# Grouped-query attention, twice, on one core: each step's maximum over all keys by a GpSimd all-reduce across partitions

## The chip, the cores and the metric

The kernel runs on one core of a Trainium2 chip. The metric is the device time of one execution, in microseconds (us), from the runs shown below. A core has five engines with queues of their own: TensorE (PE in the profile; its weight loads are PEld), VectorE (DVE), ScalarE (ACT), GpSimd (POOL) and SyncE (SP, which here only issues transfers). Each works through its instructions in the order in which they were written, and waits on semaphores for what other engines make.

## The reference

Two independent attention blocks, A and B, of the same shapes; the outputs stand side by side in the last dimension.

```python
# B, Sq, D = 16, 80, 576;  Hq, Hkv, Sk, Dh = 32, 16, 512, 128;  all bfloat16
q = (x @ wq).reshape(B, Sq, Hq, Dh).transpose(0, 2, 1, 3)
k = jnp.repeat(k_cache, 2, axis=1)          # two query heads share one key head
v = jnp.repeat(v_cache, 2, axis=1)
scores = jnp.einsum("bhqd,bhkd->bhqk", q, k) * (Dh ** -0.5)
p = softmax(scores, axis=-1)
o = jnp.einsum("bhqk,bhkd->bhqd", p, v)
return o.transpose(0, 2, 1, 3).reshape(B, Sq, Hq * Dh) @ wo
```

## The kernel before, in words

*Steps.* The work is cut into 128 steps. A step is one block (A or B), one batch row and a group of four key heads, with the eight query heads that belong to them. Its scores are 16 pieces: for each of four key heads and each quarter of the 512 keys, 128 keys on the partitions and 160 columns (two query heads of 80 queries). Three pieces share a PSUM bank, so a piece of work of the score stage is 480 columns wide, and there are 683 of them.

*Score stage.* Line 704 multiplies keys by queries into a bank. Line 710 (VectorE) takes, on each partition, the negated maximum of the bank's columns into a column of `negmax`. Line 714 (ScalarE) makes the exponentials with this as bias, into `p_sb`, which has 27 slots. So the exponentials of each partition, which is a key, have a maximum of their own, and this has to be made good before they are summed over keys.

*The weights of a step, which the change touches.* The 16 pieces of a step lie in 6 columns of `negmax`. Line 736 (VectorE) takes the minimum of these 6 on each partition, `gmin`. Line 739 (TensorE) multiplies `gmin`, repeated over 128 columns as weights, by the identity: each row of the result holds the values of all 128 partitions. Line 743 (VectorE) takes the minimum along this row, `gmn`, which is the same on all partitions: minus the maximum over all keys of the step. Line 746 (ScalarE) makes the six weights per partition, `wt`, by an exponential of `gmn` minus `negmax`. Line 749 (GpSimd) copies the weights as an 18-column strip into `vp`, which gives the sums of the softmax. Line 767 scales V by the weights into `vp`, up to six instructions a step, on GpSimd but for three in the last step (VectorE). `vp` has four slots, the weights two.

*Behind it.* Lines 800 and 819 multiply the exponentials by `vp`; line 839 takes reciprocals of the sums; lines 844 and 849 scale; line 866 transposes; lines 877 and 879 copy to `oT`; line 949 makes the output projection, and lines 961, 969 and 976 gather it. Line 607 makes the queries (from `wq`), and lines 623 and 625 copy them.

*Loads.* K comes by transposing transfers on SP's queue (line 672, five slots), V by plain ones on ScalarE's queue (line 676; the first four on SP's), asked for four steps ahead, when a slot has come free. `wo` and `wq` come on SP's queue.

*What sets the order.* A planner (class `_Sched`) gets every operation with a due time (`key`), a lead (`ahead`) and a duration (`dur`, `lat`), plays them through engine by engine, and writes down the order of each engine; at the same time it gives out PSUM banks, and for operations with two possible engines it picks one. The chip then follows this order, with semaphores between engines. An operation with another duration or on another engine therefore moves others as well. GpSimd's instructions are written for the chip in this order; configuration instructions for it are added when the program is built, and stand in no line of the kernel.

At the end a flag is read on every engine; if sums left the allowed range, a second, plain version of the whole would run. It does not run on these inputs.

Of the kernel before, what the change touches and what calls it, by code (L numbers as in the profile page):

```python
# [1 line left out]

# [3 lines left out]

BF16 = mybir.dt.bfloat16
F32 = mybir.dt.float32
I32 = mybir.dt.int32
AF = mybir.ActivationFunctionType  # L10
AX = mybir.AxisListType
# [7 lines left out]
NNM = 48  # L19
# [42 lines left out]
STENG = "sp"  # L62
STL = 6.0
TLG = 2
TLA = 4.0
TLN = 5
TLO = 4.0
# [12 lines left out]
RCO = 2.0  # L80
# [23 lines left out]
def _mm(n, cols):  # L104
    return n * (cols * MM1 + MM0)
# [271 lines left out]
def bass_concat_heads__gqa_block_cached__gqa_block_cached__near_ridge_kernel(  # L377
# [10 lines left out]
    _, G, SK, DH = A_k_cache.shape  # L388
# [15 lines left out]
    with ExitStack() as es:  # L404
        block = es.enter_context(nc.Block())
        sb = lambda name, shape, dt: es.enter_context(nc.sbuf_tensor(name, shape, dt))
        ident = sb("ident", [128, 128], BF16)
# [10 lines left out]
        osb = sb("osb", [128, NOSB, DC], BF16)  # L418
        acc = sb("acc", [128, NPP * NRT, D], F32)
        negmax = sb("negmax", [128, NNM], F32)  # L420
        gmin = sb("gmin", [128, 2], BF16)
        gmn = sb("gmn", [128, 2], F32)
        wt = sb("wt", [128, 2, 6], F32)
        rinv = sb("rinv", [128, NRI * 5], F32)
# [5 lines left out]
        ps = es.enter_context(nc.psum_tensor("ps", [128, 8, 512], F32))  # L430
# [14 lines left out]
        S = _Sched()  # L445

        def R(res, ver):
            return (res, ver)
# [37 lines left out]
        def em_warmend(e):  # L486
# [5 lines left out]
              stream="warmset")  # L492
        IDENT = R(("ident",), 0)
# [10 lines left out]
        for half in range(NPP):  # L504
            x_ap = probs[0][0]
            for part, (k0, k1) in enumerate(XP):
                def em_ldx(e, x_ap=x_ap, half=half, k0=k0, k1=k1):
# [5 lines left out]
                      writes=[R(("xs", half * NRT + k_), 0) for k_ in range(k0, k1)], dsem="d_x%d%d" % (half, part), land=LAND["x%d%d" % (half, part)],  # L513
                      name="ldx%d.%d" % (half, part), stream="first", dur=0.5, cost=XC * (k1 - k0))
            for blk in range(NRT):
# [11 lines left out]
                def em_xev(e, en=None, half=half, blk=blk, vb=vb):  # L527
# [4 lines left out]
                      stream="X", dur=_mm(5, 128), lat=0.2, alloc=[vb])  # L532
                S.add(("act", "dve") if half else "act" if blk in (1, 3) else "dve", x + 0.3, em_xev, reads=[R(vb, 0)], writes=[R(("xT", half, blk), 0)],
                      name="xev%d" % rb, stream="xed" if half else "xea" if rb in (1, 3) else "xev",
                      dur=dict(act=0.52, dve=0.40), lat=0.13)

        for half in range(NPP):
            x_ap = probs[1][0]
            st0 = UPR + 8 * half - lead[NG // 2 + half]
            for ck in range(5):  # L540
                def em_ldxt(e, x_ap=x_ap, half=half, ck=ck):
# [6 lines left out]
                      writes=[R(("xT", half, b_), 1) for b_ in range(NRT)] if ck == 0 else [R(("xT", half, "t", ck), 1)],  # L548
# [7 lines left out]
        for goct in range(NG):  # L556
# [6 lines left out]
            for pi, (c0, c1) in enumerate(pieces):  # L563
# [11 lines left out]
                for j, (k0, k1, n0, n1) in enumerate(parts):  # L575
                    def em_ldw(e, wq_ap=wq_ap, q=q, wsl=wsl, n0=n0, n1=n1, k0=k0, k1=k1):
                        if k0 == 4:
# [15 lines left out]
            for i in range(8):  # L593
                for c in range(2):
# [6 lines left out]
                    n0, n1 = b0 * SQ, (b0 + nb) * SQ  # L601
# [27 lines left out]
                    if prob:  # L629
                        xr += [R(("xT", half, "t", ck), 1) for ck in range(1, 5)]  # L630
                    S.add("pe", x, em_qp,
                          reads=[R(("wq", wsl, w_, i // 2), wv) for w_ in range(5)] + [R(("wqz",), 0)] + xr,
                          writes=[R(vb, 0)] + [R(("qT", qpos(goct, bl), i), goct) for bl in range(b0, b0 + nb)],
                          name="qp%d.%d.%d" % (goct, i, c), stream="Q" if goct > 1 else "Q%d" % goct,
                          dur=_mm(5, n1 - n0), lat=0.2, alloc=[vb])
                    S.add(("act", "dve"), x + 0.4, em_qev, reads=[R(vb, 0)],
                          writes=[R(("qT", qpos(goct, bl), i), goct) for bl in range(b0, b0 + nb)],
                          name="qev%d.%d.%d" % (goct, i, c), stream="qev" if goct > 1 else "qev%d" % goct,
                          dur=QEV[n1 - n0] if qpos(goct, b0) + nb <= NQS else QEV[n1 - n0, 2])

        for Q in range(NQ):
# [3 lines left out]
            for wc in range(NWC):  # L645
                def em_ldwo(e, wo_ap=wo_ap, h0=q * HH + wc * hc, s0=Q % 2 * HH + wc * hc, hc=hc):
# [5 lines left out]
                      writes=[R(("wo", Q % 2, wc), Q)] + ([R(("warm",), 3), R(("ones",), 1)] if Q + wc == 0 else []),  # L652
# [10 lines left out]
        for U in range(NSU):  # L663
# [10 lines left out]
            def em_ldv(e, vc_ap=vc_ap, b=b, q=q, vs=vs):  # L674
# [7 lines left out]
                  writes=[R(("V", vs), U)],  # L682
# [4 lines left out]
        for t in range(NT):  # L687
            blks = []
            for B_ in range(3 * t, min(3 * t + 3, NBK)):
                U, r_ = divmod(B_, 16)  # L690
# [22 lines left out]
            def em_exp(e, vb=vb, si=si, sl=sl, n=n):  # L713
# [3 lines left out]
                  dur=_mm(len(blks), 160), lat=0.2, alloc=[vb])  # L717
            S.add("dve", kq(t) + 0.45, em_max, reads=[R(vb, 0)], writes=[R(("nm", si), t)],
                  name="max%d" % t, stream="max", dur=0.045 + n * 0.00108, lat=0.12, ahead=MXO)
            S.add("act", kq(t) + 1.1, em_exp, reads=[R(vb, 0), R(("nm", si), t)], writes=[R(("P", sl), t)],  # L720
                  name="exp%d" % t, stream="exp", dur=0.045 + n * 0.00106, lat=0.2)
# [3 lines left out]
        for U in range(NSU):  # L725
            pi, grp = of_step[U]
            vr, vs, gs = U % NV, U % NVP, U % 2
            t0 = PT0[U]
            off = 16 * U - 3 * t0
            n0 = t0 % NNM  # L730
            kg = kq(t0 + 5)
            tla = TLA if U >= NSU - TLG else 0.0
            vbx = S.bank("X")

            def em_g(e, gs=gs, n0=n0):
                return e.tensor_reduce(gmin[:, gs:gs + 1], negmax[:, n0:n0 + 6], axis=AX.X, op=AluOpType.min)

            def em_mb(e, gs=gs, vbx=vbx):
                return e.matmul(ps[:, vbx.phys, 0:128], lhsT=gmin[:, gs:gs + 1].broadcast_to([128, 128]), rhs=ident[:],  # L739
                                start=True, stop=True)  # L740

            def em_mm(e, gs=gs, vbx=vbx):
                return e.tensor_reduce(gmn[:, gs:gs + 1], ps[:, vbx.phys, 0:128], axis=AX.X, op=AluOpType.min)  # L743

            def em_w(e, gs=gs, n0=n0, vs=vs):
                return e.activation(wt[:, gs, :], negmax[:, n0:n0 + 6], AF.Exp, bias=gmn[:, gs:gs + 1], scale=-1.0)  # L746

            def em_wc(e, gs=gs, vs=vs):
                return e.tensor_copy(vp[:, vs, :, 128:129].rearrange("p (r i) o -> p r (i o)", i=3),  # L749
# [1 line left out]

            S.add("dve", kg + 1.0, em_g, reads=[R(("nm", (t0 + i) % NNM), t0 + i) for i in range(6)],
                  writes=[R(("gm", gs), U)], name="g%d" % U, stream="g", dur=0.07, lat=0.13, ahead=RCO + tla)
            S.add("pe", kg + 1.1, em_mb, reads=[R(("gm", gs), U), IDENT], writes=[R(vbx, 0)], name="mb%d" % U,
                  stream="G", dur=_mm(1, 128), lat=0.2, alloc=[vbx], ahead=RCO + tla)
            S.add("dve", kg + 1.2, em_mm, reads=[R(vbx, 0)], writes=[R(("gn", gs), U)], name="mm%d" % U, stream="mm",
                  dur=0.2, lat=0.13, ahead=RCO + 2.0 + tla)
            S.add("act", kg + 1.3, em_w, reads=[R(("gn", gs), U)] + [R(("nm", (t0 + i) % NNM), t0 + i) for i in range(6)],
                  writes=[R(("w", gs), U)], name="w%d" % U, stream="w", dur=0.195, lat=0.15, ahead=RCO + 2.0 + tla)
            S.add("pool", kg + 1.45, em_wc, reads=[R(("w", gs), U)], writes=[R(("vp", vs, "c"), U)], name="wc%d" % U,  # L760
                  stream="vsp", dur=0.167, lat=0.1)
            for r in range(6):
# [7 lines left out]
                def em_va(e, p0=p0, p1=p1, vr=vr, vs=vs, off=off, gs=gs, r=r):  # L770
# [5 lines left out]
                      reads=[R(("w", gs), U), R(("V", vr), U)], writes=[R(("vp", vs, r), U)], name="vs%d.%d" % (U, r),  # L776
                      stream="vs" + ve, dur=dict(p=0.241 + 0.107 * (p1 - p0), d=0.3, a=0.05 + 0.13 * (p1 - p0))[ve],
                      lat=0.1, ahead=0.0 if ve == "p" else 3.0)

            if U == grp[0]:  # L780
                gn = len(grp)
# [10 lines left out]
            for u in range(4):  # L792
# [3 lines left out]
                def em_pv(e, u=u, vo=vo, c0=c0, vs=vs, where=where):  # L796
# [10 lines left out]
                    reads=[R(("P", (t0 + r_) % NPS), t0 + r_) for r_ in rs_] + [R(("vp", vs, r_), U) for r_ in rs_ + ["c"]],  # L807
                    writes=[R(vo, 0)], name="pv%d.%d" % (U, u), stream="PV", dur=_mm(4, 129), lat=0.2,
                    alloc=[vo] if m_ % 3 == 0 else [])
# [3 lines left out]
            def em_pr(e, od=oba[-1], pair=tuple(pair)):  # L813
                last = None
                for h_, (U_, vs_, t0_, where_) in enumerate(pair):
# [10 lines left out]
                  reads=[R(("P", (t0_ + r_) % NPS), t0_ + r_) for _, _, t0_, _ in pair for r_ in range(6)]  # L826
                  + [R(("vp", vs_, r_), U_) for U_, vs_, _, _ in pair for r_ in [0, 1, 2, 3, 4, 5, "c"]],
                  writes=[R(oba[-1], 0)], name="pr%d" % U, stream="PV", dur=0.225 * gn, lat=0.2, mode=1, alloc=[oba[-1]])
# [5 lines left out]
            for h_, (a_, b_, xo) in enumerate(parts_):  # L834
# [6 lines left out]
                def em_on(e, en, pi=pi, r0=r0, vo=vo, a_=a_, b_=b_):  # L841
# [6 lines left out]
                    for k in range(a_, b_):  # L848
# [5 lines left out]
                      stream="rcp", dur=0.08, lat=0.13, ahead=RCO + tlo)  # L854
# [66 lines left out]
        def em_flag(e, vf=vf):  # L921
# [4 lines left out]
              stream="chk", dur=0.1)  # L926
# [269 lines left out]
```

## Time and profile before

| what | value |
|---|---|
| median of 2 runs | 698.87 us (698.3 to 699.44) |
| profiled execution, its own time | 699.79 us |
| its span, first to last instruction | 698.0 us |
| TensorE clock granted | 1.000 |
| bytes moved by DMA | 160.78 MB, mean 230 GB/s |
| read from HBM | 87.46 MB |

The span is what the profile's views divide up; 1.8 us of the profiled execution's time lie around it. A row of a group gives line, engine, operation, what is written from what, the shape and the count, then after the bar the busy time in us, the mean of one in ns, after the next bar the idle time of the engine just before these instructions, and what ended it. Busy times of one engine can overlap by a little, since an instruction may start before the record of the one ahead of it has ended. Matmul ends are modelled, and spans on GpSimd are rough.

### The profile page before, as it was taken

How to read it: one execution, taken by the hardware profiler on the slowest of the kernel's cores; microseconds unless marked ns; L12 is line 12 of the kernel's file. 1: busy time of each engine (PE TensorE's matmuls, PEld its weight loads, DVE VectorE, ACT ScalarE, POOL GpSimd, SP SyncE). 2: the span in 40 equal slices, each digit the busy share in tenths (PEclk: the TensorE clock that was granted, in tenths of full speed). 3: DMA queues.
4: the chain of work that ended last, by engine and by line, in shares of the span. 5: the costliest groups of instructions: out<-in, count | busy, mean ns of one | idle time of the engine just before them, and what ended most of it. 6: DMA issues, size and time to landing. Idle time of an engine off the chain costs nothing.

```text
span 698.0 us, 23763 instructions
## 1 busy us (share of the span) xinstructions
PE 687.7 (99%) x9533; PEld 581.0 (83%) x9533; DVE 650.2 (93%) x1656; ACT 603.8 (86%) x1365; POOL 428.5 (61%) x901
## 2 busy tenths in 40 slices
PE   8999999999999999999999999999999999999996
PEld 5778888888888888888888888888888888888885
DVE  5899889899999999999999999999999999999995
ACT  2778799799999888899989999999898989988893
POOL 1465466656666666567666575666766667675572
PEclk9999999999999999999999999999999999999999
DMA  9999999999999999999999999999999999999951
GB/s 242 210 276 249 258 235 278 223 180 234 244 231 251 231 246 284 225 248 241 243 225 239 253 240 254 234 253 236 226 226 250 231 226 239 222 249 208 197 138 39
DMA packets 362837, 160.78 MB, mean 230 GB/s; under 512 B 276832, under 2 KB 359264, under 8 KB 362720
## 3 DMA queue, kind: packets, MB, share of 16 engines
q1 hardware_dynamic: 297168, 94.10, 76.0%
q10 hardware_dynamic: 65552, 65.09, 31.4%
q8 instruction: 77, 1.26, 0.7%
q14 instruction: 40, 0.33, 0.2%
HBM read 87.46 MB, written 2.95 MB: 130 GB/s over the span
## 4 chain that ended last, share of the span: by engine, by line
PE 89%; DVE 6%; ACT 2%; SPq 2%; DMA 1%; issue 0%
PE ps L607 23%; PE ps L949 21%; PE ps L704 19%; PE ps L800 16%; PE ps L866 5%; PE ps L819 4%; DVE negmax L710 4%; SPq L672 1%; PE ps L739 1%; ACT p_sb L714 1%; DMA acc<-in_A_x_dram 1%; DVE acc L969 0%; ACT o_sb L849 0%; DVE osb L976 0%; DVE o_sb L844 0%
## 5 line engine op out<-in xcount | busy, mean ns | idle before, releaser
L714 ACT ACTIVATE p_sb<-ps,negmax 128x480 bf16<-128x480 f32 (+1 forms) x683 | 421.6, 680 | 46.1 <-DVE negmax L710 43.4
L710 DVE TENSOR_REDUCE negmax<-ps 128x1 f32<-128x480 f32 (+1 forms) x683 | 418.3, 646 | 7.2 <-PE ps L704 6.1
L767 POOL TENSOR_SCALAR vp<-v_sb,wt 128x384 bf16<-128x384 bf16 (+2 forms) x765 | 405.5, 555 | 0.0
L704 PE MATMUL ps<-qT,kT 128*128 128x160 bf16 x2048 | 235.4, 232 | 0.2 <-ACT p_sb L714 0.2
L607 PE MATMUL ps<-xT,wq_sb 128*128 128x320 bf16 (+2 forms) x1280 | 212.2, 299 | 1.4 <-DVE xT L528 0.6
L800 PE MATMUL ps<-vp,p_sb 128*128 128x129 bf16 x2048 | 193.6, 220 | 0.5 <-DVE oT L877 0.2
L749 POOL CAST vp<-wt 128x18 bf16<-128x18 f32 x128 | 33.8, 264 | 258.1 <-ACT wt L746 257.8
L949 PE MATMUL ps<-wo_sb,oT 128*128 128x288 bf16 x1280 | 190.7, 286 | 0.1
L704 PEld LDWEIGHTS ps<-qT,kT 128*128 128x128 bf16 x2048 | 157.4, 97 | 18.3 <-ACT p_sb L714 0.4
L800 PEld LDWEIGHTS ps<-vp,p_sb 128*128 128x128 bf16 x2048 | 142.9, 98 | 10.2 <-DVE oT L877 0.4
L607 PEld LDWEIGHTS ps<-xT,wq_sb 128*128 128x128 bf16 x1280 | 115.3, 98 | 36.0 <-DVE wo_sb L487 0.9
L949 PEld LDWEIGHTS ps<-wo_sb,oT 128*128 128x128 bf16 x1280 | 117.6, 98 | 24.3 <-ACT p_sb L714 0.3
L849 ACT ACTIVATE o_sb<-ps,rinv 128x128 bf16<-128x128 f32 x343 | 101.7, 379 | 5.3 <-DVE rinv L839 4.4
L625 DVE TENSOR_SCALAR qT<-ps 128x320 bf16<-128x320 f32 (+4 forms) x192 | 82.7, 442 | 9.0 <-PE ps L607 7.4
L844 DVE TENSOR_TENSOR o_sb<-ps,rinv 128x384 bf16<-128x384 f32 x100 | 54.8, 548 | 1.5
L877 ACT COPY oT<-ps 128x640 bf16<-128x640 bf16 (+2 forms) x70 | 45.2, 670 | 7.2 <-PE ps L866 6.8
L866 PE MATMUL ps<-ident,o_sb 128*128 128x128 bf16 x640 | 50.2, 219 | 0.6 <-ACT oT L877 0.3
L746 ACT ACTIVATE wt<-negmax,gmn 128x6 f32<-128x6 f32 x128 | 40.3, 315 | 9.0 <-DVE gmn L743 8.3
L866 PEld LDWEIGHTS ps<-ident,o_sb 128*128 128x128 bf16 x640 | 39.8, 98 | 4.1 <-ACT o_sb L849 0.7
L623 ACT ACTIVATE qT<-ps 128x320 bf16<-128x320 f32 (+3 forms) x88 | 37.4, 432 | 6.5 <-PE ps L607 6.0
L969 DVE TENSOR_TENSOR acc<-ps,acc 128x288 f32<-128x288 f32 x80 | 36.1, 451 | 4.8 <-PE ps L949 4.1
L839 DVE RECIPROCAL rinv<-ps 128x3 f32<-128x3 f32 (+1 forms) x216 | 35.7, 169 | 5.2 <-PE ps L800 2.5
(36 smaller groups left out, 259.1 us busy)
## 6 DMA issues: line engine op xcount, KB each, us to landing
v_sb<-in_B_v_cache_dram ACTq DMA_DIRECT2D x64, 512.0 KB, 5.6
v_sb<-in_A_v_cache_dram ACTq DMA_DIRECT2D x60, 512.0 KB, 5.6
wo_sb<-in_A_wo_dram SPq DMA_DIRECT2D x16, 288.0 KB, 5.5
wo_sb<-in_B_wo_dram SPq DMA_DIRECT2D x16, 288.0 KB, 5.7
wq_sb<-in_B_wq_dram SPq DMA_DIRECT2D x16, 256.0 KB, 4.9
out_dram<-osb SPq DMA_DIRECT2D x40, 72.0 KB, 3.8
wq_sb<-in_A_wq_dram SPq DMA_DIRECT2D x4, 512.0 KB, 5.6
v_sb<-in_A_v_cache_dram SPq DMA_DIRECT2D x4, 512.0 KB, 5.6
```

What stands on the lines that cost most here:

```text
L607: last = e.matmul(ps[:, vb.phys, 0:n1 - n0], lhsT=wq_sb[:, wsl, ck, i * 128:(i + 1) * 128], rhs=xT[:, half, ck, n0:n1], start=(ck == 0), s ...
L625: r_ = e.tensor_scalar(dst, src[:, s0:s0 + n_, :], SCALE, None, op0=AluOpType.mult)
L704: last = e.matmul(ps[:, vb.phys, i * 160:(i + 1) * 160], lhsT=kT[:, U % NK, j, u * 128:(u + 1) * 128], rhs=qT[:, qpos(U // 8, U % 8), u * ...
L710: return e.tensor_reduce(negmax[:, si:si + 1], ps[:, vb.phys, 0:n], axis=AX.X, op=AluOpType.max, negate=True)
L714: return e.activation(p_sb[:, sl, 0:n], ps[:, vb.phys, 0:n], AF.Exp, bias=negmax[:, si:si + 1], scale=1.0)
L767: return e.tensor_scalar(vp[:, vs, p0:p1, 0:128], src, wt[:, gs, r:r + 1], 1.0, op0=AluOpType.mult, op1=AluOpType.mult)
L800: last = e.matmul(ps[:, vo.phys, c0:c0 + 129], lhsT=p_sb[:, sl, i * 160:i * 160 + 128], rhs=vp[:, vs, p_, 0:129], start=(j == 0), stop=(j ...
L844: return e.tensor_tensor(o_sb[:, pi % NOS, a_:b_, :], src[:, :, 0:128], rinv[:, r0 + a_:r0 + b_].unsqueeze(2).broadcast_to([128, b_ - a_, ...
L849: last = e.activation(o_sb[:, pi % NOS, k, :], src[:, k - a_, 0:128], AF.Identity, scale=rinv[:, r0 + k:r0 + k + 1])
L866: last = e.transpose(dst, o_sb[:, pi % NOS, 4 * h2 + k if k < 4 else 4 * gn + h2, :], ident[:])
L877: r_ = cp(oT[:, :, g0:g0 + n_], src[:, :, 0:n_])
L949: last = e.matmul(ps[:, vb.phys, 0:DC], lhsT=oT[:, hi, p0:p0 + 128], rhs=wo_sb[:, w0 + hi, c3 * DC:(c3 + 1) * DC], start=(hi == 0), stop=( ...
```

## The change

Line 736 now writes the negated minimum of the six columns, as float32 (`gmax`), that is, the maximum on each partition. In place of the matmul stands a GpSimd instruction, an all-reduce across the 128 partitions with the maximum, from `gmax` to `gall`. In place of VectorE's reduction of the matmul's result, VectorE adds `gall` to the six columns of `negmax` (`dm`), and the exponential reads `dm` with no bias. The operation is planned on GpSimd with a duration of `ARD`, and no PSUM bank is asked for. The planner writes the order of every engine anew. In the changed kernel the lines stand at 738 (reduction), 741 (all-reduce), 744 (addition), 747 (exponential), 750 (copy) and 768 (scaling of V).

```diff
+ARD = 1.0
...
-        gmin = sb("gmin", [128, 2], BF16)
+        gmax = sb("gmax", [128, 2], F32)
+        gall = sb("gall", [128, 2], F32)
+        dm = sb("dm", [128, 2, 6], F32)
...
-            vbx = S.bank("X")
...
-                return e.tensor_reduce(gmin[:, gs:gs + 1], negmax[:, n0:n0 + 6], axis=AX.X, op=AluOpType.min)
+                return e.tensor_reduce(gmax[:, gs:gs + 1], negmax[:, n0:n0 + 6], axis=AX.X, op=AluOpType.min, negate=True)
...
-                return e.matmul(ps[:, vbx.phys, 0:128], lhsT=gmin[:, gs:gs + 1].broadcast_to([128, 128]), rhs=ident[:],
-                                start=True, stop=True)
+                return e.partition_all_reduce(gall[:, gs:gs + 1], gmax[:, gs:gs + 1], 128, bass_isa.ReduceOp.max)
...
-                return e.tensor_reduce(gmn[:, gs:gs + 1], ps[:, vbx.phys, 0:128], axis=AX.X, op=AluOpType.min)
+                return e.tensor_scalar(dm[:, gs, :], negmax[:, n0:n0 + 6], gall[:, gs:gs + 1], None, op0=AluOpType.add)
...
-                return e.activation(wt[:, gs, :], negmax[:, n0:n0 + 6], AF.Exp, bias=gmn[:, gs:gs + 1], scale=-1.0)
+                return e.activation(wt[:, gs, :], dm[:, gs, :], AF.Exp, scale=-1.0)
...
-            S.add("pe", kg + 1.1, em_mb, reads=[R(("gm", gs), U), IDENT], writes=[R(vbx, 0)], name="mb%d" % U,
-                  stream="G", dur=_mm(1, 128), lat=0.2, alloc=[vbx], ahead=RCO + tla)
-            S.add("dve", kg + 1.2, em_mm, reads=[R(vbx, 0)], writes=[R(("gn", gs), U)], name="mm%d" % U, stream="mm",
-                  dur=0.2, lat=0.13, ahead=RCO + 2.0 + tla)
+            S.add("pool", kg + 1.1, em_mb, reads=[R(("gm", gs), U)], writes=[R(("ga", gs), U)], name="mb%d" % U,
+                  stream="mb", dur=ARD, lat=0.15, ahead=RCO + 2.0)
+            S.add("dve", kg + 1.2, em_mm, reads=[R(("ga", gs), U)] + [R(("nm", (t0 + i) % NNM), t0 + i) for i in range(6)],
+                  writes=[R(("gn", gs), U)], name="mm%d" % U, stream="mm", dur=0.08, lat=0.13, ahead=RCO + 2.0 + tla)
```

More of the change, by code (lines that the diff above doesn't have):

```diff
@@ L3 @@
 import concourse.bass as bass
-from concourse import mybir
+from concourse import bass_isa, mybir
 from concourse.alu_op_type import AluOpType
@@ L732, in bass_concat_heads__gqa_block_cached__gqa_block_cached__near_ridge_kernel, with em_mb, em_mm @@
             tla = TLA if U >= NSU - TLG else 0.0
-            vbx = S.bank("X")
             def em_g(e, gs=gs, n0=n0):
-                return e.tensor_reduce(gmin[:, gs:gs + 1], negmax[:, n0:n0 + 6], axis=AX.X, op=AluOpType.min)
-            def em_mb(e, gs=gs, vbx=vbx):
-                return e.matmul(ps[:, vbx.phys, 0:128], lhsT=gmin[:, gs:gs + 1].broadcast_to([128, 128]), rhs=ident[:],
-                                start=True, stop=True)
-            def em_mm(e, gs=gs, vbx=vbx):
-                return e.tensor_reduce(gmn[:, gs:gs + 1], ps[:, vbx.phys, 0:128], axis=AX.X, op=AluOpType.min)
+                return e.tensor_reduce(gmax[:, gs:gs + 1], negmax[:, n0:n0 + 6], axis=AX.X, op=AluOpType.min, negate=True)
+            def em_mb(e, gs=gs):
+                return e.partition_all_reduce(gall[:, gs:gs + 1], gmax[:, gs:gs + 1], 128, bass_isa.ReduceOp.max)
+            def em_mm(e, gs=gs, n0=n0):
+                return e.tensor_scalar(dm[:, gs, :], negmax[:, n0:n0 + 6], gall[:, gs:gs + 1], None, op0=AluOpType.add)
             def em_w(e, gs=gs, n0=n0, vs=vs):
-                return e.activation(wt[:, gs, :], negmax[:, n0:n0 + 6], AF.Exp, bias=gmn[:, gs:gs + 1], scale=-1.0)
+                return e.activation(wt[:, gs, :], dm[:, gs, :], AF.Exp, scale=-1.0)
             def em_wc(e, gs=gs, vs=vs):
@@ L753, in bass_concat_heads__gqa_block_cached__gqa_block_cached__near_ridge_kernel @@
                   writes=[R(("gm", gs), U)], name="g%d" % U, stream="g", dur=0.07, lat=0.13, ahead=RCO + tla)
-            S.add("pe", kg + 1.1, em_mb, reads=[R(("gm", gs), U), IDENT], writes=[R(vbx, 0)], name="mb%d" % U,
-                  stream="G", dur=_mm(1, 128), lat=0.2, alloc=[vbx], ahead=RCO + tla)
-            S.add("dve", kg + 1.2, em_mm, reads=[R(vbx, 0)], writes=[R(("gn", gs), U)], name="mm%d" % U, stream="mm",
-                  dur=0.2, lat=0.13, ahead=RCO + 2.0 + tla)
-            S.add("act", kg + 1.3, em_w, reads=[R(("gn", gs), U)] + [R(("nm", (t0 + i) % NNM), t0 + i) for i in range(6)],
+            S.add("pool", kg + 1.1, em_mb, reads=[R(("gm", gs), U)], writes=[R(("ga", gs), U)], name="mb%d" % U,
+                  stream="mb", dur=ARD, lat=0.15, ahead=RCO + 2.0)
+            S.add("dve", kg + 1.2, em_mm, reads=[R(("ga", gs), U)] + [R(("nm", (t0 + i) % NNM), t0 + i) for i in range(6)],
+                  writes=[R(("gn", gs), U)], name="mm%d" % U, stream="mm", dur=0.08, lat=0.13, ahead=RCO + 2.0 + tla)
+            S.add("act", kg + 1.3, em_w, reads=[R(("gn", gs), U)],
                   writes=[R(("w", gs), U)], name="w%d" % U, stream="w", dur=0.195, lat=0.15, ahead=RCO + 2.0 + tla)
```

## The prediction

> **What bounds the kernel now.** I read the page's engine shares first, then the chain that ended last, then the waits, and then the groups of the lines that the change touches.
>
> ```profile
> span 698.0 us, 23763 instructions
> PE 687.7 (99%) x9533; PEld 581.0 (83%) x9533; DVE 650.2 (93%) x1656; ACT 603.8 (86%) x1365; POOL 428.5 (61%) x901
> POOL 1465466656666666567666575666766667675572
> PE 89%; DVE 6%; ACT 2%; SPq 2%; DMA 1%; issue 0%
> PE ps L607 23%; PE ps L949 21%; PE ps L704 19%; PE ps L800 16%; PE ps L866 5%; PE ps L819 4%; DVE negmax L710 4%; SPq L672 1%; PE ps L739 1%; ACT p_sb L714 1%; DMA acc<-in_A_x_dram 1%; DVE acc L969 0%; ACT o_sb L849 0%; DVE osb L976 0%; DVE o_sb L844 0%
> ```
>
> TensorE is busy for 99% of the span and holds 89% of the chain; VectorE follows at 93%. GpSimd is busy for 61% and isn't on the chain at all. What it waits for is a single thing:
>
> ```profile
> POOL vp L749 <- ACT wt L746: 257.8, 109, 22.3
> ```
>
> These 257.8 us, less the 22.3 us before its first step, are its slack: (257.8 - 22.3) / 128 = 1.8 us in each of the 128 steps. The change spends from this slack. One step's chain as it is now stands in the timeline (start, length, line):
>
> ```profile
> 345.66 0.16 DVE L736 TENSOR_REDUCE gmin<-negmax 128x1 bf16<-128x6 f32 x1
> ...
> 345.88 0.23 PE L739 MATMUL ps<-ident,gmin 128*128 128x128 bf16 x1
> ...
> 346.22 0.28 DVE L743 TENSOR_REDUCE gmn<-ps 128x1 f32<-128x128 f32 x1
> ...
> 346.54 0.30 ACT L746 ACTIVATE wt<-negmax,gmn 128x6 f32<-128x6 f32 x1
> ...
> 346.90 0.26 POOL L749 CAST vp<-wt 128x18 bf16<-128x18 f32 x1 [0.58 <-ACT wt L746]
> ```
>
> From the minimum to GpSimd's copy it takes 1.24 us, and TensorE's part is one matmul among others.
>
> **The change, part by part.** The groups that it removes or replaces, and GpSimd's own work:
>
> ```profile
> L767 POOL TENSOR_SCALAR vp<-v_sb,wt 128x384 bf16<-128x384 bf16 (+2 forms) x765 | 405.5, 555 | 0.0
> L746 ACT ACTIVATE wt<-negmax,gmn 128x6 f32<-128x6 f32 x128 | 40.3, 315 | 9.0 <-DVE gmn L743 8.3
> L743 DVE TENSOR_REDUCE gmn<-ps 128x1 f32<-128x128 f32 x128 | 35.9, 280 | 0.7 <-PE ps L739 0.7
> L749 POOL CAST vp<-wt 128x18 bf16<-128x18 f32 x128 | 33.8, 264 | 258.1 <-ACT wt L746 257.8
> L739 PE MATMUL ps<-ident,gmin 128*128 128x128 bf16 x128 | 28.3, 221 | 0.0
> L736 DVE TENSOR_REDUCE gmin<-negmax 128x1 bf16<-128x6 f32 x128 | 19.0, 148 | 0.2
> ```
>
> *Removed:* 128 matmuls of 0.221 us, 28.3 us at most of TensorE's 687.7. The VectorE reduction over 128 columns (0.280 us) becomes an operation on 6 columns, priced like L736 (0.148): 128 x 0.132 = 17 us less. ScalarE's exponential keeps its shape (0.315). One PSUM bank per step comes free. All of it is a gain only while those engines set the pace.
>
> *Added on GpSimd, the all-reduce:* 128 instructions on one column. The trace has none. The nearest rows are GpSimd's own: the copy above, and the spread of line 767 (shortest, median and longest in ns):
>
> ```profile
> L767 POOL TENSOR_SCALAR vp<-v_sb,wt x765: 370/589/647, 25.6 to 686.6; 128x384 bf16<-128x384 bf16 x150, 128x128 bf16<-128x128 bf16 x21, 128x256 bf16<-128x256 bf16 x21
> ```
>
> That is 0.264 us for 18 columns and 0.647 us for the longest tensor_scalar. I take 0.45, about the middle, because it folds partitions and is more than a copy, and keep 0.26 and 0.65: 57.6 us, from 33 to 83.
>
> *Added on GpSimd, what the diff doesn't show:* the built program's order on GpSimd, here from the middle (rows by number, with their waits; line 741 is the all-reduce, 768 the scaling of V):
>
> ```
> 474 L741 ISA
> 475 L741 ISA gall<-gmax 128x1 [waits e_dve]
> 476 L750 TensorCopy vp<-wt 128x18 [waits e_act]
> 477 L768 ISA
> 478 L768 TensorScalarPtr vp<-v_sb,wt 128x2x128 [waits d_v3]
> ```
>
> An instruction without operands stands ahead of the all-reduce, and another ahead of the first tensor_scalar after it. Over the kernel there are 125 of each, 250 together (three times two all-reduces follow each other under one). The kernel before has this kind only twice on GpSimd, once ahead of the affine_select at line 454, where the profile names it:
>
> ```profile
> 0.78 0.20 POOL L451 MEMSET wo_sb<- 128x128 bf16 x1 [0.29 <-POOLq L1181]
> 1.06 0.29 POOL L454 TENSOR_SCALAR_AFFINE_SELECT ident<-wo_sb 128x128 bf16<-128x128 bf16 x1
> ```
>
> ```profile
> L454 POOLq MODIFY_POOL_CONFIG x2: 11/11/11, 0.9 to 1.0; - x2
> ```
>
> So GpSimd is reconfigured from one set of operations to the other and back in every step. That the order alternates strictly says that the two sets don't stand in GpSimd at the same time, so I take each switch to be a transfer into GpSimd with a drain before and a start behind it. Its price isn't in this trace. From below: the one switch there is took 11 ns and nothing waited, which is a case of nothing to fetch, and is a rival below. As a transfer, the nearest rows are those of the DMA issues (median us from issue to landing):
>
> ```profile
> v_sb<-in_B_v_cache_dram ACTq DMA_DIRECT2D x64, 512.0 KB, 5.6
> kT<-in_B_k_cache_dram SPq DMA_TRANSPOSE x64, 7.7
> wq_sb<-in_A_wq_dram ACTq DMA_DIRECT2D x1, 64.0 KB, 3.4
> ...
> DMA packets 362837, 160.78 MB, mean 230 GB/s; under 512 B 276832, under 2 KB 359264, under 8 KB 362720
> ```
>
> Its size is unknown; I take the commonest plain row, 5.6, plus the 0.29 us that GpSimd stood idle behind its queue's work at line 451: 5.9 us. The ends are 3.4 (the shortest, nothing added) and 7.7 + 0.29 = 8.0. The Trainium skill, "GPSIMD Engine Reference", section 2.1, states that the first call to a freshly loaded kernel pays a code load of about 6 us (5.95 measured) that shows as no instruction of its own; by it the sum below would be 249 x 0.05 = 12 us higher. No run shown here has such a load.
>
> Two switches of 5.9 us a step against 1.8 us of slack: GpSimd becomes the bound, and the sum is its own time. The stretches that I use, and where it starts:
>
> ```profile
> 0.00:26.00 26.00, 22.65 (x188) 14.46 (x189) 16.39 (x36) 9.97 (x16) 3.05 (x10) 1.00 1.00 231
> 26.00:686.00 660.00, 658.32 (x9267) 561.39 (x9265) 628.67 (x1604) 591.46 (x1346) 424.19 (x890) 1.00 1.10 234
> 686.00:698.00 12.00, 6.69 (x83) 5.11 (x81) 5.12 (x19) 2.38 (x5) 1.24 (x3) 0.98 0.14 38
> ```
>
> ```profile
> 23.31 0.15 DVE L736 TENSOR_REDUCE gmin<-negmax 128x1 bf16<-128x6 f32 x1
> ...
> 685.64 1.60 POOL L767 TENSOR_SCALAR vp<-v_sb,wt 128x256 bf16<-128x256 bf16 x3
> ```
>
> (The columns of the windows are length, PE, PEld, DVE, ACT, POOL, clock, DMA, GB/s.)
> - Until the first step's maximum is there: 23.31 + 0.15 = 23.5 us. The first switch lies in this time and is free.
> - 249 switches x 5.9 = 1469.1.
> - 128 all-reduces x 0.45 = 57.6.
> - Its work as now: 424.19 + 1.24 = 425.4.
> - Waits that stay. Where the copy of line 750 follows the all-reduce directly (47 of the 128 steps, by the order), nothing hides the way over VectorE and ScalarE; in 78 others a switch and scalings stand between. From VectorE's start to the copy it takes 346.90 - 346.22 = 0.68 us now: 47 x 0.7 = 33 (none to twice that, as ScalarE's queue stands).
> - From GpSimd's last work to the end: 698.0 - (685.64 + 1.60) = 10.8.
>
> Together 2019.4; the profiled execution's time is 699.79, 1.8 over its span, which gives 2021. That execution is 0.9 us over the median of 698.87, which I neglect.
>
> What queues behind: the all-reduce waits for line 738's result on VectorE, and behind it on GpSimd stand scalings of the step before, which TensorE's products (line 801) need. VectorE's line 744 waits for the all-reduce with later maxima behind it, and ScalarE's line 747 with later exponentials. These cost nothing as long as the switches cover them: a step of 15.8 us (2021 / 128) holds TensorE's 5.1 us (658.32 / 128), and VectorE and ScalarE have less. V's load of 5.6 us is asked for when a slot comes free, four slots deep. With the work spread over three times the span, DMA needs 230 x 699 / 2021 = 80 GB/s.
>
> A rule that speaks against such gaps. The row first: the clock granted to TensorE is 1.00 in the long window, since its work never stops. The Trainium skill, "TensorE: Matmul & The Clock Gate", Part 1, says that an idle window of some 3.4 us halves it. By it TensorE would need 2 x 5.1 = 10.3 us a step, still under 15.8, and the sum would grow only behind GpSimd's last work, by the last window's 6.7 us.
>
> **The rivals.**
> 1. *Switches cost nothing* (the other side). What was fetched stays, or is fetched under other work; for it: 11 ns at line 454 and no gap there. Then GpSimd's step is 428.5 / 128 + 0.45 = 3.8 of 5.45 us, still hidden, and the kernel is TensorE's: between 699 - 28.3 = 671 and no change, some 685. It decides below (1.8 - 0.45) / 2 = 0.7 us a switch. Against it: with no need to fetch, no second switch would have to stand in every step.
> 2. *Cheap switches, dear all-reduce.* A fold over 128 partitions might take microseconds. It counts from 1.8 us on; at 4 us the time is 699 + 128 x (4 - 1.8) = 981. Against it: no GpSimd row on this many columns is over 0.65 us.
> 3. *Dearer switches.* The code goes to several cores, or waits behind transfers; at 12 us: 2021 + 249 x 6.1 = 3540. Against it: the DMA queues empty out as the kernel slows.
>
> **How the numbers follow.** A switch within 3.4 to 8.0 us: 0.84. Its ends: 23.5 + 249 x 3.4 + 33 + 425 + 33 + 10.8 + 1.8 = 1374, and 23.5 + 249 x 8.0 + 83 + 425 + 66 + 10.8 + 1.8 + 6.7 = 2609. Rival 1: 0.05, of which 0.03 is faster by over 2% and 0.02 within it (2% is about what a measurement of this kernel tells from no change). Rival 2: 0.03. Rival 3: 0.08. The range is that of the first case, 1370 to 2610; it leaves 0.16 out. Slower: 0.84 + 0.03 + 0.08 = 0.95. The time is 2020.
>
> **What would show it.** Right: GpSimd's own queue (line 741 and 768) holds over half of the chain, gaps of 5 to 6 us stand on GpSimd ahead of each all-reduce and each first scaling behind it, TensorE is busy near 35%, and the step is about 15.8 us. The all-reduce itself under 0.65 us. Wrong: a gap on GpSimd under 0.7 us with TensorE still on the chain (rival 1), a long all-reduce without gaps (rival 2), or gaps that differ from 5.9, which moves the time by 249 times the difference; also gaps that wait for VectorE or ScalarE, which I put at 33 us in all.

## The result, and the profile after

| what | before | after |
|---|---|---|
| median of 2 runs | 698.87 us | 2266.09 us (2263.56 to 2268.62) |
| ratio, 95% interval | | 3.230 (3.208 to 3.251) |
| profiled execution, its own time | 699.79 us | 2263.56 us |
| its span | 698.0 us | 2261.7 us |
| TensorE clock granted, mean | 1.000 | 0.683 |

The change makes the kernel 3.2 times as slow. The time lies inside the forecast range of 1370 to 2610 us, 12% above the 2020 us. In the measurements of the experiments the kernel before also has executions with a lower clock and a longer time; the ratios given below leave these out.

The page of the changed kernel answers the page shown for the kernel before: engine shares, GpSimd's busy tenths, the granted clock (in tenths of full speed) and the chain by engine.

```profile
span 2261.7 us, 24006 instructions
PE 963.6 (43%) x9405; PEld 754.0 (33%) x9405; DVE 689.6 (30%) x1678; ACT 596.9 (26%) x1278; POOL 480.7 (21%) x1029
POOL 1221222222212222212222222122212221212211
PEclk8666766776676666677676676666766676667676
issue 60%; PE 23%; DVE 7%; POOL 7%; ACT 1%; SPq 1%; POOLq 0%; DMA 0%
```

No engine is busy for even half of the span, and GpSimd, which sets the pace, is busy for 21%. A reader who looks for the bound among the busy shares finds nothing. The chain tells it: 60% of it is "issue", time in which an engine waited for nothing that the profile shows. The waits say where (engine and line, what it waited for, us in total, times, longest):

```profile
PE ps L801 <- POOL vp L768: 1177.7, 123, 19.8
...
POOL vp L768 <- issue: 923.6, 125, 9.3
POOL gall L741 <- issue: 775.9, 121, 8.6
...
DVE dm L744 <- POOL gall L741: 523.3, 123, 13.1
```

GpSimd stands still 125 times ahead of a scaling of V and 121 times ahead of an all-reduce, as often as the built program has switches there, less four ahead of an all-reduce: the first ran out under the wait for the first maximum, and three gaps end on a result of VectorE. TensorE and VectorE then wait for GpSimd. One step on GpSimd's timeline (start, length, line, idle before it in brackets):

```profile
1016.74 0.38 POOL L741 PARTITION_ALL_REDUCE gall<-gmax  x1 [5.87 <-issue]
1024.21 2.06 POOL L768 TENSOR_SCALAR vp<-v_sb,wt 128x384 bf16<-128x384 bf16 x4 [7.09 <-issue]
1026.23 0.26 POOL L750 CAST vp<-wt 128x18 bf16<-128x18 f32 x1
1026.41 2.72 POOL L768 TENSOR_SCALAR vp<-v_sb,wt 128x256 bf16<-128x256 bf16 x5
1035.77 0.38 POOL L741 PARTITION_ALL_REDUCE gall<-gmax  x1 [6.65 <-issue]
```

An all-reduce of 0.38 us has a gap of some 6 us before it and one of some 7 us behind it. The copy of line 750 has no gap behind a scaling, and where it directly follows an all-reduce the built program has no switch between them: not every operation belongs to one of the two sets. The switches themselves stand in the rows of their lines, at almost no length:

```profile
L741 POOLq MODIFY_POOL_CONFIG  x250: 1/3/10, 3.3 to 2232.2; - x125
L741 POOL PARTITION_ALL_REDUCE gall<-gmax x128: 351/378/382, 23.5 to 2238.0; - x128
```

(Shortest, median and longest in ns; each switch leaves two records.) So the record of such an instruction says nothing of its price. The price is the gap behind it.

### The profile page after: what moved, and what is told of

Its sections match the earlier page's. It is cut to its first block, busy times and chain, and to the rows that moved or that the text cites. A ratio compares the mean times of both kernels' runs of the same rounds, so it can differ in the third digit from the quotient of the medians.

```text
span 2261.7 us, 24006 instructions
## 1 busy us (share of the span) xinstructions
PE 963.6 (43%) x9405; PEld 754.0 (33%) x9405; DVE 689.6 (30%) x1678; ACT 596.9 (26%) x1278; POOL 480.7 (21%) x1029
## 2 busy tenths in 40 slices
DMA packets 362840, 160.79 MB, mean 71 GB/s; under 512 B 276832, under 2 KB 359264, under 8 KB 362720
## 4 chain that ended last, share of the span: by engine, by line
issue 60%; PE 23%; DVE 7%; POOL 7%; ACT 1%; SPq 1%; POOLq 0%; DMA 0%
PE ps L801 7%; PE ps L950 5%; PE ps L610 5%; PE ps L707 5%; POOL vp L768 4%; DVE negmax L713 4%; POOL gall L741 2%; PE ps L820 1%; PE ps L867 1%; DVE o_sb L845 1%; DVE qT L628 1%; DVE dm L744 0%; POOL vp L750 0%; ACT wt L747 0%; DVE acc L970 0%
## 5 line engine op out<-in xcount | busy, mean ns | idle before, releaser
L801 PE MATMUL ps<-vp,p_sb 128*128 128x129 bf16 x2048 | 263.8, 274 | 1177.7 <-POOL vp L768 1177.7
L768 POOL TENSOR_SCALAR vp<-v_sb,wt 128x384 bf16<-128x384 bf16 (+2 forms) x765 | 406.5, 543 | 923.6 <-issue 923.6
L801 PEld LDWEIGHTS ps<-vp,p_sb 128*128 128x128 bf16 x2048 | 190.6, 123 | 1235.7 <-POOL vp L768 1137.0
L707 PE MATMUL ps<-qT,kT 128*128 128x160 bf16 x2048 | 298.2, 280 | 62.2 <-ACT p_sb L717 59.5
L610 PE MATMUL ps<-xT,wq_sb 128*128 128x320 bf16 (+2 forms) x1280 | 277.3, 362 | 27.8 <-DVE acc L970 7.8
L950 PE MATMUL ps<-wo_sb,oT 128*128 128x288 bf16 x1280 | 244.7, 337 | 7.6 <-DVE qT L628 2.9
L707 PEld LDWEIGHTS ps<-qT,kT 128*128 128x128 bf16 x2048 | 207.7, 121 | 96.5 <-ACT p_sb L717 67.1
L741 POOL PARTITION_ALL_REDUCE gall<-gmax x128 | 48.3, 377 | 816.6 <-issue 775.9
L744 DVE TENSOR_SCALAR dm<-negmax,gall 128x6 f32<-128x6 f32 x128 | 29.4, 230 | 523.4 <-POOL gall L741 523.3
L950 PEld LDWEIGHTS ps<-wo_sb,oT 128*128 128x128 bf16 x1280 | 141.1, 116 | 48.3 <-DVE qT L628 3.7
L850 ACT ACTIVATE o_sb<-ps,rinv 128x128 bf16<-128x128 f32 x245 | 72.1, 367 | 132.3 <-DVE rinv L840 129.8
L845 DVE TENSOR_TENSOR o_sb<-ps,rinv 128x384 bf16<-128x384 f32 (+2 forms) x133 | 72.8, 548 | 1.8
```

The source lines that it names most:

```text
L610: last = e.matmul(ps[:, vb.phys, 0:n1 - n0], lhsT=wq_sb[:, wsl, ck, i * 128:(i + 1) * 128], rhs=xT[:, half, ck, n0:n1], start=(ck == 0), s ...
L707: last = e.matmul(ps[:, vb.phys, i * 160:(i + 1) * 160], lhsT=kT[:, U % NK, j, u * 128:(u + 1) * 128], rhs=qT[:, qpos(U // 8, U % 8), u * ...
L741: return e.partition_all_reduce(gall[:, gs:gs + 1], gmax[:, gs:gs + 1], 128, bass_isa.ReduceOp.max)
L768: return e.tensor_scalar(vp[:, vs, p0:p1, 0:128], src, wt[:, gs, r:r + 1], 1.0, op0=AluOpType.mult, op1=AluOpType.mult)
L801: last = e.matmul(ps[:, vo.phys, c0:c0 + 129], lhsT=p_sb[:, sl, i * 160:i * 160 + 128], rhs=vp[:, vs, p_, 0:129], start=(j == 0), stop=(j ...
L845: return e.tensor_tensor(o_sb[:, pi % NOS, a_:b_, :], src[:, :, 0:128], rinv[:, r0 + a_:r0 + b_].unsqueeze(2).broadcast_to([128, b_ - a_, ...
```

## The experiments

Three theories were to be told apart. S: the switches make the time, by their number and their price. A: the all-reduce itself holds GpSimd, in time that the profile shows as idle. H: the longer way in every step, from VectorE over GpSimd and back, makes the time.

**A copy in place of the all-reduce.** The same instruction stands at the same place with the same waits, but it is one that needs no switch.

```diff
-                return e.partition_all_reduce(gall[:, gs:gs + 1], gmax[:, gs:gs + 1], 128, bass_isa.ReduceOp.max)
+                return e.tensor_copy(gall[:, gs:gs + 1], gmax[:, gs:gs + 1])
```

> The all-reduce is replaced by a GpSimd copy of the same column (each partition keeps its own maximum, so the weights are not the reference's); order, waits and hand-overs stay, the switches of GpSimd's set of operations go. Theory S (the 250 switches make the time, 6.2 us toward the all-reduce and 7.2 us back): TensorE sets the pace again, 680 to 705 us, with TensorE over 95% busy. Theory H (the longer way from VectorE over GpSimd and back in every step makes the time, and the gaps on GpSimd are parts of it): the way is as long as before, so over 1500 us.

Measured: 0.999 of the kernel before, 95% interval 0.993 to 1.005; in the profile TensorE is busy for 96% of the span. All of the loss is gone with the hand-overs unchanged, so H falls. H would have had to explain 1567 us; the hand-overs, together with the matmuls taken off TensorE, change the time by less than 1% either way. A is not touched by this run, since the all-reduce went together with the switches.

**All-reduces without switches.** GpSimd scales V by copies, so that nothing calls for the other set.

```diff
-                    return e.tensor_scalar(vp[:, vs, p0:p1, 0:128], src, wt[:, gs, r:r + 1], 1.0,
-                                           op0=AluOpType.mult, op1=AluOpType.mult)
+                    return e.tensor_copy(vp[:, vs, p0:p1, 0:128], src)
```

> All 128 all-reduces stay; the scaling of V on GpSimd is replaced by plain copies of V of the same shapes (the weights are left out of the products, only the sums have them), which need no switch back, so one switch is left in the whole kernel. Theory S: 128 x 0.38 us of all-reduce fit in GpSimd's slack: 680 to 720 us, unless the copies are dearer than the scalings. Theory A (the all-reduce holds GpSimd for microseconds that the profile shows as idle): 128 x 6.4 us stay, over 1400 us. Theory H: over 1500 us.

Measured: 718.71 us in one run, beside runs of the kernel before of 699.58 to 730.73 on the same chip. One run doesn't tell whether a per cent or two of loss are left; it does rule out the 1400 us and more of A and H. In its profile the all-reduces, the switches that are left, and the waits for them are

```profile
L741 POOL PARTITION_ALL_REDUCE gall<-gmax x128 | 45.5, 356 | 145.7 <-DVE gmax L738 129.0 <-DVE rinv L839 16.2
...
L741 POOLq MODIFY_POOL_CONFIG  x2: 1/1/1, 12.9 to 13.0; - x2
...
POOL ident L457 <- issue: 9.6, 1, 9.6
...
L527 PE MATMUL ps<-ident,acc 128*128 128x128 bf16 x50 | 4.2, 241 | 6.1 <-POOL ident L457 6.1
```

All 128 all-reduces are there, 0.356 us each, and GpSimd waits ahead of them only for VectorE's results. The whole dearness of the all-reduce is its switch: A falls. Two switches are left, not one. That of line 741 lies under the wait for the first maximum. The other stands ahead of the affine_select of line 457; GpSimd waits 9.6 us for it, beside the first loads (245 GB/s in the page's first slice), and TensorE's first transposes wait 6.1 us, which is part of this kernel's time.

The kernel before and the changed one have a configuration instruction at this place too, with gaps of 0.1 and 0.3 us. What differs is the set that each execution leaves behind: these two end on a tensor_scalar, while this one stays with the all-reduce's set from line 741 on. The two kernels of GpSimd alone further down fit: the one that ends on all-reduces begins with an all-reduce without a gap (at 2.29 us), the one that ends on tensor_scalars begins with an all-reduce behind a gap of 5.93. So the set seems to stay in place from one execution to the next, and a configuration instruction for the set that is in place seems to cost nothing. That reading is from these traces alone; no run was made for it.

**Two all-reduces in a row.**

```diff
+                e.partition_all_reduce(gdup[:, gs:gs + 1], gmax[:, gs:gs + 1], 128, bass_isa.ReduceOp.max)
                 return e.partition_all_reduce(gall[:, gs:gs + 1], gmax[:, gs:gs + 1], 128, bass_isa.ReduceOp.max)
```

> A second all-reduce of the same column stands directly behind the first in every step, in the same set of operations, so with no further switch. Theory S: 128 x 0.38 us more, 2266 + 49 = 2315 us. Theory A (each all-reduce brings the gap of 6.4 us ahead of it): 2266 + 128 x 6.8 = 3130 us.

Measured: 2303.69 us in one run, 38 more than the changed kernel's median. The old instruction's group (line 743) and the new one's (line 742, the first of the two):

```profile
L743 POOL PARTITION_ALL_REDUCE gall<-gmax x128 | 54.2, 424 | 0.0
L742 POOL PARTITION_ALL_REDUCE gdup<-gmax x128 | 48.2, 377 | 815.0 <-issue 774.9 <-DVE gmax L739 28.3 <-DVE rinv L842 6.0
```

The first of the two has all of the idle time before it, the second none. The 38 us are 0.30 us for each instruction added, without a gap (A had 864 us). The two profiles agree: the span is 40 us longer and GpSimd's busy time 44 us, while its idle time ahead of both lines is the same within 4 us. That the added work shows in the time at all tells that GpSimd is the bound: in the slack of the kernel before it would have been free.

**Half of the switches.**

```diff
+                if U_ % 2:
+                    return e.tensor_copy(gall[:, gs:gs + 1], gmax[:, gs:gs + 1])
                 return e.partition_all_reduce(gall[:, gs:gs + 1], gmax[:, gs:gs + 1], 128, bass_isa.ReduceOp.max)
```

> Steps of even number keep the all-reduce, odd ones have the copy (left out: their maximum over partitions). 128 switches in place of 250. Theory S: 23.5 + 127 x 6.8 + 64 x 0.38 + 64 x 0.25 + 425 + waits 60 + 13 = 1425 us. Theory H: within 5% of 2266 us, since every step still goes over GpSimd.

Measured: 1574.77 us in one run. The time goes with the number of switches, as S has it, but it is 150 us over my sum. GpSimd's waits:

```profile
POOL vp L770 <- issue: 469.6, 64, 8.7
POOL gall L743 <- issue: 433.3, 62, 9.8
POOL vp L752 <- ACT wt L749: 123.3, 85, 3.9
POOL gall L742 <- DVE gmax L738: 40.5, 31, 3.5
POOL gall L743 <- DVE gmax L738: 26.5, 2, 20.0
```

A switch costs (469.6 + 433.3) / 126 = 7.17 us here, against 6.91 in the changed kernel ((923.6 + 775.9) / 246). That is 127 x 0.37 = 47 us over the 6.8 that I took. Nearly all of it is in the direction toward the all-reduce, 433.3 / 62 = 6.99 against 775.9 / 121 = 6.41; the faster kernel moves its bytes at 102 GB/s in the mean, the changed one at 71. The waits on ScalarE and VectorE, without the 20 us before the first step, are 170 us, where I took 60: in the steps without a switch nothing covers the way over the other engines.

**The switches alone.** A kernel of GpSimd's alone; the loads come from SP's queue.

```python
for i in range(30):      # quiet; then again beside plain loads, then beside transposing loads
    e.partition_all_reduce(g_out[...], g_in[:, 0:1], 128, bass_isa.ReduceOp.max)
    e.tensor_scalar(dst[...], src[:], g_in[:, 0:1], 1.0, op0=AluOpType.mult, op1=AluOpType.mult)
```

> None of the reference is computed. GpSimd alternates 30 times between an all-reduce and a tensor_scalar of 384 columns with nothing else on the chip, then 30 times beside plain loads of 512 KB (four under way), then 30 times beside transposing loads, then does 30 all-reduces in a row. Theory D (the spread of 5.7 to 9.3 us, and the 0.9 us over my 5.9, come from other transfers): quiet, both directions 5 us or less, and 1 us or more longer beside the loads. Theory F (a switch has a fixed price, other transfers add only the spread): quiet 5.7 toward the all-reduce and 6.7 back, as the shortest in the changed kernel, and beside the loads the medians 6.2 and 7.2. The all-reduces in a row: 0.38 us each or less.

Measured, in GpSimd's waits (lines 37 and 38 quiet; 42 and 43 beside plain loads; 47 and 48 beside transposing ones; the first of each pair is the all-reduce; line 52 the all-reduces in a row):

```profile
POOL dst L43 <- issue: 225.2, 30, 9.9
POOL dst L48 <- issue: 220.5, 30, 8.5
POOL dst L38 <- issue: 211.5, 30, 7.7
POOL g_out L42 <- issue: 191.9, 30, 7.5
POOL g_out L47 <- issue: 188.9, 30, 7.6
POOL g_out L37 <- issue: 172.0, 29, 6.3
POOL g_out L52 <- issue: 5.8, 1, 5.8
```

Quiet, a switch is 172.0 / 29 = 5.93 us toward the all-reduce and 211.5 / 30 = 7.05 back. The 30 all-reduces in a row have one gap and take 0.33 us each, under the 0.38 expected. The loads of the second part lasted for only 188 of its some 440 us, so its mean hides their effect. The windows (length, GpSimd's busy time, clock, DMA share, GB/s) and GpSimd's timeline within the loads show it:

```profile
412.00:600.00 188.00, 11.09 (x24) 1.00 1.08 340
600.00:846.00 246.00, 16.75 (x36) 1.00 0.04 13
```

```profile
478.97 0.58 POOL L43 TENSOR_SCALAR dst<-src,g_in 128x384 bf16<-128x384 bf16 x1 [8.43 <-issue]
486.55 0.38 POOL L42 PARTITION_ALL_REDUCE g_out<-g_in  x1 [7.01 <-issue]
495.32 0.57 POOL L43 TENSOR_SCALAR dst<-src,g_in 128x384 bf16<-128x384 bf16 x1 [8.39 <-issue]
503.05 0.38 POOL L42 PARTITION_ALL_REDUCE g_out<-g_in  x1 [7.16 <-issue]
```

Beside 340 GB/s a switch is some 7.0 and 8.3 us in the mean of that window. Both theories of the spread hold in part: there is a fixed price of 5.9 and 7.0 us, which no quiet brings to 5 (against D), and 1.1 to 1.2 us on top while the transfers are dense, which is more than F had.

**Other operations across the same switch.** The alternation once more in quiet, with an iota in place of the tensor_scalar (lines 39 and 40), then with a partition broadcast in place of the all-reduce (lines 44 and 45).

```diff
-                e.tensor_scalar(dst[...], src[:], g_in[:, 0:1], 1.0, op0=AluOpType.mult, op1=AluOpType.mult)
+                e.iota(it[:, i, :], [[1, 64]], base=0, channel_multiplier=0)
...
-                e.partition_all_reduce(g_out[...], g_in[:, 0:1], 128, bass_isa.ReduceOp.max)
+                e.partition_broadcast(pb[:, i, :], g_in[0:1, 0:1], 128)
```

> None of the reference is computed; the chip is quiet. GpSimd alternates 30 times between an all-reduce and an iota of 64 columns, then 30 times between a partition broadcast and a tensor_scalar of 384 columns. Theory F1 (the price belongs to the set that is put in place): ahead of all-reduce and broadcast 5.9 us, ahead of iota and tensor_scalar 7.0 us. Theory F2 (it belongs to the operation that follows): iota and broadcast differ from tensor_scalar and all-reduce by more than 0.5 us.

```profile
POOL it L40 <- issue: 211.8, 30, 7.6
POOL dst L45 <- issue: 210.3, 30, 7.7
POOL pb L44 <- issue: 176.6, 30, 6.2
POOL g_out L39 <- issue: 176.4, 30, 6.1
```

7.06 and 7.01 us ahead of iota and tensor_scalar, 5.89 and 5.88 ahead of broadcast and all-reduce: F1. For these four operations the price belongs to the set that is put in place, not to the operation that follows. Why one set costs 1.1 us more was not tried.

**Without the maximum over all keys, a try at a faster kernel.** From the kernel before, lines 736 to 743 are taken out, and the weights become

```diff
-                return e.activation(wt[:, gs, :], negmax[:, n0:n0 + 6], AF.Exp, bias=gmn[:, gs:gs + 1], scale=-1.0)
+                return e.activation(wt[:, gs, :], negmax[:, n0:n0 + 6], AF.Exp, scale=-1.0)
```

The factor that all keys of a step have in common goes out in the division by the sums; the flag at the end still sends sums out of range to the plain version.

> Made from the kernel before: the maximum over all keys is left out, the weights are the exponentials of each partition's own maxima, and the common factor goes out in the division by the sums; the flag at the end guards the range as before. 128 matmuls of 0.22 us go from TensorE, two reductions (0.15 and 0.28 us) per step from VectorE. If TensorE's busy time is what counts: 699 - 28 = 671 us. If VectorE's 93% held part of the pace too, down to 660. If the re-planned order eats the gain: 685 to 700.

> The kernel without the maximum over all keys once more, for a closer interval. If TensorE's 28 us count in full, 0.96 of the kernel before; if the first run's middle holds, 0.99.

Measured: 0.990 (0.979 to 1.000), and in the longer measurement 0.998 (0.994 to 1.002). So the matmul, both reductions and all hand-overs of this part together are worth nothing that can be measured here, and by the longer measurement 0.7% at most. This is no faster version.

**The same with less of V loaded.** Both the kernel before and this one, with a quarter of each load of V.

```diff
+                if U_ >= NVS:
+                    return e.dma_start(v_sb[:, vs, 0:1, :], src[:, 0:1, :])
                 return e.dma_start(v_sb[:, vs, :, :], src)
```

> The kernel before, with a quarter of each load of V from the fifth step on (three of four key heads keep old values of V): 48 MB less to move. If the loads share the pace of the kernel before: 2% or more under it. If not: within 1%.

> The kernel without the maximum over all keys, with the same quarter loads of V. Theory L (the gain of taking the matmul and the reduction out was lost to late transfers of K and V): 28 us or so under the kernel before with quarter loads, some 660 to 675. Theory P (the gain is lost in the order of the engines): the same as the kernel before with quarter loads, within 1%.

Measured: 0.9993 (0.9979 to 1.0007), median 699.6 us, and 0.984 (0.981 to 0.987), median 689.4 us. The loads do not hold back the kernel before. Without the maximum, 10 us appear once the loads are thinned. In the profile of that kernel with full loads (700.02 us) TensorE waits 4.4 us for K, with the thinner loads not at all. It is also busy for 3.2 us longer there, at a granted clock of 0.994 against 0.999, so the runs do not tell the loads' part from the clock's. Even so the gain is 10 us and not 28, so neither theory holds: L had the full 28, P none. TensorE's busy time in the two profiles, the kernel before with less V and then the one without the maximum with less V:

```profile
PE 687.5 (98%) x9533; PEld 580.9 (83%) x9533; DVE 650.3 (93%) x1656; ACT 603.8 (86%) x1365; POOL 428.8 (61%) x901
```

```profile
PE 677.0 (98%) x9405; PEld 577.2 (84%) x9405; DVE 638.0 (93%) x1444; ACT 569.1 (83%) x1280; POOL 429.7 (62%) x901
```

128 matmuls less are 10.5 us less: 0.08 us each, not the 0.221 of their records. (The order was planned anew as well, so the 0.08 is not exact.) In the timeline of the kernel before, matmuls of a like size overlap (4 and 3 of them):

```profile
340.12 0.40 PE L800 MATMUL ps<-vp,p_sb 128*128 128x129 bf16 x4
340.36 0.37 PE L704 MATMUL ps<-qT,kT 128*128 128x160 bf16 x3
```

One record is 0.22 us, four in a row take 0.40: each further one adds 0.06.

## Why the prediction was right, and where it was off

The mechanism, the direction and the range held; the size of one term was off. GpSimd's waits in the changed kernel, ahead of line 741 and then ahead of line 750 (us, times):

```profile
  issue: 775.9, 121
  DVE gmax L738: 28.7, 5
  DVE negmax L713: 6.1, 1
  DVE rinv L840: 5.8, 1
```

```profile
  ACT wt L747: 27.2, 44
```

Of the waits on VectorE, 20.1 us lie before the first step and 6.5, 6.1 and 5.8 are whole switches, whose end fell together with VectorE's result. The profiled execution's 2263.56 us, term by term against the sum on record:

| term | forecast, us | measured, us | from |
|---|---|---|---|
| until the first all-reduce | 23.5 | 23.5 | timeline: the first one at 23.46 |
| switches | 1469.1 | 1718 | 923.6 + 775.9, and 18.4 in three gaps that end on VectorE |
| all-reduces | 57.6 | 48.3 | 128 x 0.377 |
| GpSimd's other work | 425.4 | 430 | windows, less the all-reduces and the first 23.5 us |
| waits that stay | 33 | 29 | 27.2 on ScalarE, 28.7 - 20.1 - 6.5 on VectorE |
| behind GpSimd's last work | 10.8 | 12.7 | from 2248.97 to 2261.7 |
| outside the span | 1.8 | 1.9 | 2263.56 - 2261.7 |

*Finding the bound.* Right: GpSimd's slack of 1.8 us a step was the number that counted, and the built program's order, not the diff, showed what would fill it. With copies in their place, the time came back to 0.999.

*The price of a switch.* This is the step that was mis-sized: 5.9 us forecast, 1718 / 249 = 6.9 measured. That makes 249 us, against a miss of 242 us in all; the other terms' misses, from -9 to +5 us, add up to about -7. I had worked it out as the landing of one transfer of 512 KB plus 0.29 us. No run shows that a switch is such a transfer: the page counts 160.79 MB where the kernel before has 160.78, so 250 switches leave no bytes in it. That the sum came so near the quiet 5.93 is luck in part. The runs show 5.9 in quiet only for the direction toward the all-reduce; back it is 7.05, and I had made no difference between the two. Their mean of 6.49 accounts for 147 us of the 249; the other 102 us are 0.41 us a switch. The changed kernel's own trace says that its transfers add them: the gaps in which no bytes moved have a mean of 5.91 us toward the all-reduce (23 of 121) and 7.09 back (47 of 125), as on the quiet chip though the other engines work, and the quarter with the most traffic has 7.01 (at 204 GB/s) and 7.80 (at 126). The Trainium skill's 5.95 us ("GPSIMD Engine Reference", section 2.1) agrees with the quiet switch toward the all-reduce, and with its word that no instruction of its own shows the load; the switch back is longer than it says.

*The all-reduce.* 0.45 us taken, 0.377 measured, inside the ends. It lies nearer to GpSimd's copy (0.264) than to its longest scaling.

*What queues behind.* Right in size: all waits on other engines together are 29 us. (The low end of the range took them at 33, although the forecast allowed for none; with none it would be 1341.) They are covered in the changed kernel, and they come out when the cover goes, as the kernel with half of the switches shows (170 us). Off the path two prices were wrong and cost nothing: line 744 took 0.230 us where I had 0.148, and the exponential of line 747 took 0.208 where I had kept 0.315.

*TensorE's clock.* The clock did fall, from 1.00 to 0.68 of full speed in the mean, with matmuls of line 801 at 0.274 us in the mean against 0.220, and waits of 9.6 us ahead of them (1177.7 / 123). TensorE's busy time became 935.64 / 128 = 7.3 us a step between GpSimd's first and last work, where it had 5.1. It cost little, as forecast: GpSimd's gaps and work add up to the span without it. The fall beside such gaps agrees with the Trainium skill, "TensorE: Matmul & The Clock Gate", Part 1, in direction.

*The signs.* The gaps are 6.4 and 7.4 us in the mean, not 5 to 6; the step is 17.7 us (2263.56 / 128), not 15.8. TensorE is busy for 43%, not 35%: its records are longer, as said above. Lines 741 and 768 do not hold half of the chain by name: they have 6%, and the gaps stand in it as "issue", under no line.

*The rivals.* Free switches were rival 1, for gaps under 0.7 us; the shortest in the changed kernel is 5.7. What spoke for it, 11 ns and no gap at line 454, has the reading given under the second experiment: the set was probably in place already. The time that I gave it, some 685 us, was wrong as well: with the switches out the re-planned kernel stands at 0.999 of the kernel before, and with the whole part out at 0.998. I had counted each matmul of TensorE by the length of its record. Rival 2 fell with the all-reduces that run at 0.356 us without switches, rival 3 with the switches that stay under 10 us.

## What to carry to other kernels

Look at the built program's order as well as at the diff: an operation that belongs to another set of GpSimd's operations brings a switch before it and one behind it, here 5.9 and 7.0 us and more beside transfers, and neither stands in the source, nor does its record in the profile show the price. Before work is moved to an engine with slack, divide the slack by the steps: 40% of idle time was 1.8 us a step, and two switches need 13.8. And price a matmul that is to go by what a row of such matmuls takes, divided by their number, not by the length of one record.

## What the runs showed of the hardware that was not expected

- A switch of GpSimd's set has a direction: 5.88 to 5.93 us toward the set of all-reduce and broadcast, 7.01 to 7.06 us toward that of tensor_scalar and iota, on a quiet chip.
- Beside plain loads of 340 GB/s the same switches take some 7.0 and 8.3 us.
- The first configuration instruction of an execution has no gap behind it (0.1 to 0.3 us) in kernels that end on the same set, and 5.9 or 9.6 us in two that end on the other. This is read from the traces and was not tried.
- An all-reduce of one column over 128 partitions takes 0.36 to 0.42 us (0.33 us each in a row), about as much as a scaling of 128 columns (0.377 in the kernel before).
- In the kernel before, 48.8 MB of loads less (160.78 to 112.02) change the time by less than 0.3%, though DMA's share in its long window is 1.10.
